# Unit 0's second-layer steps mixed with its last four first-layer steps, and another spread of steps over slots 6, 7 and 8

## The chip, the cores and the metric

The kernel runs on one core of one Trainium2 chip. The metric is the device time of one execution in microseconds (us), taken as the median of several runs. Inputs are float32, the output is float32; inside, matmul operands are float16 and sums are float32.

The engines are named as the profile names them: PE is the matrix engine (PEld its weight loads), ACT does activations, DVE elementwise work, POOL masks and issues loads, SP issues stores and transposing transfers. Each engine works through its own list of instructions in order; between engines there are only semaphores. PSUM is the accumulator memory that PE writes and ACT and DVE read.

## The reference

The reference is an attention with a forget gate, followed by a two-layer MLP on its result:

```python
scores = scale * q @ k.T + (cum_i - cum_j)      # cum: cumulative sum of log f; causal mask
attn   = softmax(scores); y = attn @ v           # 8 batches x 8 heads, 576 positions, head size 64
x = y, heads side by side                        # 4608 tokens x 512
h = x @ w_in; g = h - tanh(h); out = g @ w_out   # 512 -> 2048 -> 512
```

## The kernel before

**Units and slots.** Attention is done by head pairs: 8 batches x 4 pairs, numbered 0 to 31 (batch 0 has pairs 0 to 3, batch 1 pairs 4 to 7, and so on). The MLP is done in nine units of 512 tokens. Batch 0 (pairs 0 to 3) is computed first by a prologue of its own. From then on `slot(p, take)` (L626) does the scores of pair p, the values of pair p-1, and `take` steps of the MLP between them. The list `mlp` (L591) holds all MLP steps in the order in which they are taken, and `TAKE` (L747) says how many each slot takes, from slot 4 on. Nothing reorders the instructions afterwards: every engine's queue is the order in which the code emits them.

**A slot.** `att_items` (L602) gives its items: seven tiles of scores, s0 to s6 (`scores`, L347: matmuls into a PSUM tile `ps`, exp on ACT into `e`, a mask on POOL); after s0 the transposes of the next pair's q (`trans`, L245, "q"), after s1 the values of the pair before ("v": 30 matmuls into `av`, then on DVE `rs` twice and `xn`, L392 to L394, and two transposing transfers on SP into `XR`, L401 and L403), after s3 the transposes of the next pair's k ("k"); in slot 7 these two come later, after s2 and s4. `trans` writes one PSUM tile, which is copied into `QT` or `KT` (L261 on ACT, L263 on DVE). s3 is a small tile of 64 columns per head, `el`. LOADS adds transfers, issued from POOL (v, q and k of later batches) or SP.

After each item the slot brings the count of MLP steps up to its share: with 10 items that count, step number i*take/10, rounded down, is reached after item i. For takes of 3 and 4 below slot 8 a table, `FEW`, names the items after which one step is taken.

**Buffers that matter here.** The score tiles `ps` have two PSUM buffers, `av` one, the tile "tr" (transposes; for k of batch 1 the pool below) one. The pool `ps_m` has three: they hold `hps` (first layer), `ops` (second layer) and k's transposes of batch 1.

**The MLP steps of units 0 and 1.** `mlp1` (L440) is a first-layer step: for unit 0 it has 8 matmuls of 256 columns (L448; two hidden blocks of 128 by half of the unit's tokens), then `gate` (L412): tanh on ACT (L414) and an add on DVE (L415) into `gt`. For unit 0, steps 0 to 3 and 8 to 11 make all hidden blocks of the first 256 tokens, steps 4 to 7 and 12 to 15 those of the last 256. `mlp2` (L575) is a second-layer step: 4 matmuls of 512 columns (L581) that add to an `ops` tile of 128 tokens; four steps make a tile, after which ACT copies it to `ost` (L585) and SP stores it (L587). So second-layer steps 0 to 7 (the first 256 tokens) need first-layer steps 0 to 3 and 8 to 11 only, step 10 needs first-layer steps 12 and 13, step 11 needs 14 and 15. From unit 2 on the second layer has another form (`seven`, L518), which is not touched.

Four steps are taken before slot 4. Slots 4 to 9 take 4, 4, 4, 3, 10 and 9. So slots 4, 5 and 6 hold first-layer steps 4 to 15 of unit 0, slot 7 three second-layer steps, slot 8 ten, and slot 9 the last three of unit 0 and the first of unit 1.

Of the kernel before, what the change touches and what calls it, by code (L numbers as in the profile page):

```python
# [22 lines left out]
def kernel(  # L23
# [25 lines left out]
    NFT = DFF // P  # L49
# [538 lines left out]

    pairs = [(b, c) for b in range(B) for c in range(NPAIR)]

    mlp = [(fn, u, s) for u in range(2) for fn in (mlp1, mlp2) for s in range(NFT)]  # L591
    mlp += [(fn, u, s) for u in range(2, NU) for fn, n in ((mlp1, NFT), (seven, 14)) for s in range(n)]
    done = [0]

# [31 lines left out]
    def slot(p, take):  # L626
        items = att_items(p)
        whole, n, base = sum(c != "" for _, c in items), 0, goal[0]
        for i, (emit, what) in enumerate(items):
            emit()  # L630
            if take in FEW and p < 2 * NPAIR:
                if what in FEW[take] and not (what == "s1" and p > NPAIR) or what == "v":
                    step()
                continue
            n += what != ""
            upto(base + n * take // whole)
        goal[0] = base + take
        upto(goal[0])
# [105 lines left out]
    norm0(4)  # L744
    step()
    goal[0] = done[0]
    TAKE = [4, 4, 4, 3, 10, 9] + 7 * [8] + 4 * [8, 7, 8, 7]  # L747
    for p in range(NPAIR, len(pairs) + 1):
        slot(p, TAKE[p - NPAIR])
        if p == NPAIR:  # L750
# [30 lines left out]
```

## Time and profile before

| what | value |
|---|---|
| median of 3 runs | 346.69 us (346.17 to 346.78) |
| the profiled execution's own time | 347.59 us |
| its span, first to last instruction | 345.9 us |
| mean granted PE clock | 0.999 |
| busy share PE, PEld, DVE, ACT, POOL | 97%, 68%, 68%, 64%, 46% |
| bytes moved | 45.96 MB, mean 133 GB/s |

The profile is of one execution. Busy times of matmuls are modelled and overlap their successors by their last part; so a PE without idle time starts one group of matmuls a little before the row of the group before it ends, and the pace of PE is read from starts. The chain of waits follows the execution back from its end to what released each step. A wait is put down to the releaser that came last. In timeline rows the columns are: start, duration, engine, line, operation, result and operands, shape, count of merged instructions, and in brackets the idle time before it and its releaser.

### The profile page before, as it was taken

The numbers are of one execution on the slowest core, as the hardware profiler recorded it, in microseconds if no ns is written. First come the engines' busy times: TensorE is split into PE (matmuls) and PEld (weight loads), VectorE is DVE, ScalarE is ACT, GpSimd is POOL, SyncE is SP. The second block draws the span as 40 slices with busy tenths as digits, with TensorE's granted clock in tenths as the row PEclk, the third lists the DMA queues.
The fourth block names the chain that finished last, engine by engine and source line by source line (L and its number), as shares of the span: only waits on it lengthen the run. The fifth ranks groups of instructions, "written<-read, shape, count | busy, mean of one in ns | idle before, by whom it ended". The sixth has DMA issues, their size and how long they took to land.

```text
span 345.9 us, 8688 instructions
## 1 busy us (share of the span) xinstructions
PE 335.6 (97%) x3354; PEld 235.6 (68%) x3354; DVE 236.2 (68%) x481; ACT 222.7 (64%) x417; POOL 158.6 (46%) x318
## 2 busy tenths in 40 slices
PE   7999998999999999999999999999999999999995
PEld 3879875554555557888886568756887786486485
DVE  7486888447953498648854796378637865975973
ACT  4687986448755787568756875687568843623631
POOL 8976358655276626655486547752222210000000
PEclk9999999999999999999999999999999999999999
DMA  9999999999999999999899999998430013002002
GB/s 90 141 201 187 204 200 163 143 147 192 158 133 141 205 151 159 136 182 167 170 160 195 176 165 161 185 170 177 101 110 17 19 50 108 3 30 93 0 32 91
DMA packets 161323, 45.96 MB, mean 133 GB/s; under 512 B 141506, under 2 KB 159234, under 8 KB 161282
## 3 DMA queue, kind: packets, MB, share of 16 engines
q0 software_dynamic: 100128, 18.36, 77.8%
q1 hardware_dynamic: 61074, 26.99, 39.5%
q8 instruction: 26, 0.43, 0.5%
q14 instruction: 15, 0.12, 0.1%
q10 hardware_dynamic: 80, 0.07, 0.1%
HBM read 36.85 MB, written 9.44 MB: 134 GB/s over the span
## 4 chain that ended last, share of the span: by engine, by line
PE 86%; DVE 6%; ACT 3%; DMA 2%; issue 1%; ACTq 0%; DVEq 0%
PE hps L462 31%; PE cx L503 13%; PE cz L503 10%; PE ps L358 10%; PE ops L581 8%; PE av L386 7%; PE hps L448 2%; PE ps L300 2%; DMA XR<-xn 2%; DVE gt L415 1%; PE t L272 1%; DVE KT L263 1%; ACT e L305 1%; ACT e L367 1%; DMA snap<-in_f_dram 1%
## 5 line engine op out<-in xcount | busy, mean ns | idle before, releaser
L462 PE MATMUL hps<-XR,win 128*128 128x512 f16 (+4 forms) x640 | 125.9, 336 | 0.5 <-DMA XR<-xn 0.3
L415 DVE TENSOR_TENSOR gt<-hps,th 128x512 f16<-128x512 f32 x144 | 98.4, 688 | 39.1 <-ACT th L414 38.0
L367 ACT ACTIVATE e<-ps 128x512 f16<-128x512 f32 x168 | 98.5, 594 | 40.0 <-PE ps L358 38.6
L414 ACT ACTIVATE th<-hps 128x512 f32<-128x512 f32 x144 | 86.1, 598 | 29.5 <-PE hps L462 20.2
L377 POOL TENSOR_SCALAR_AFFINE_SELECT e<-e 128x128 f16<-128x128 f16 x162 | 55.4, 343 | 106.6 <-ACT e L367 106.1
L462 PEld LDWEIGHTS <-win 128*128 128x128 f16 x640 | 56.3, 97 | 43.7 <-issue 0.5
L358 PE MATMUL ps<-QT,KT 67*128 67x512 f16 (+1 forms) x336 | 68.8, 277 | 1.2 <-ACT e L367 0.7
L503 PEld LDWEIGHTS <-gt 128*128 128x128 f16 x560 | 52.5, 97 | 8.3 <-DVE gt L415 0.4
L358 PEld LDWEIGHTS <-KT 67*128 67x128 f16 x336 | 31.9, 98 | 22.2 <-issue 1.1
L95 POOL DMA_DIRECT2D vn<-in_v_dram x40 | 34.2, 858 | 5.1 <-DMA win<-in_moe_w_in_dram 2.0
L581 PE MATMUL ops<-wout,gt 128*128 128x512 f16 x128 | 32.6, 378 | 0.0
L386 PEld LDWEIGHTS <-e 128*128 128x128 f16 x784 | 28.0, 97 | 3.6
L496 DVE TENSOR_TENSOR snap<-cz,snap 128x512 f32<-128x512 f32 x21 | 14.5, 691 | 22.4 <-PE cz L503 7.4
L386 PE MATMUL av<-vn,e 128*128 128x65 f16 x784 | 29.2, 193 | 0.0
L503 PE MATMUL cz<-wout,gt 128*128 128x256 f16 x224 | 27.8, 272 | 0.0
L394 DVE TENSOR_TENSOR xn<-av,rs 128x640 f16<-128x640 f32 x28 | 23.1, 825 | 1.0
L503 PEld LDWEIGHTS <-sw 128*128 128x128 f16 x224 | 21.0, 97 | 3.9
L106 POOL DMA_DIRECT2D qn<-in_q_dram x25 | 21.4, 855 | 1.7 <-issue 1.7
L106 POOL DMA_DIRECT2D kn<-in_k_dram x25 | 21.4, 855 | 1.2 <-issue 1.2
L540 ACT ACTIVATE snap<-cx 128x512 f32<-128x512 f32 (+1 forms) x16 | 8.7, 544 | 16.2 <-PE cx L503 16.2
L581 PEld LDWEIGHTS <-gt 128*128 128x128 f16 x128 | 11.1, 97 | 10.6 <-issue 0.5
L305 ACT ACTIVATE e<-ps 128x512 f16<-128x512 f32 x25 | 14.4, 596 | 5.2 <-PE ps L303 3.2
(108 smaller groups left out, 378.5 us busy)
## 6 DMA issues: line engine op xcount, KB each, us to landing
vn<-in_v_dram POOLq DMA_DIRECT2D x32, 128.0 KB, 6.3
out_dram<-ost SPq DMA_DIRECT2D x14, 256.0 KB
out_dram<-snap SPq DMA_DIRECT2D x14, 256.0 KB
qn<-in_q_dram POOLq DMA_DIRECT2D x24, 128.0 KB, 5.8
kn<-in_k_dram POOLq DMA_DIRECT2D x24, 128.0 KB, 4.2
QT<-TQ SPq DMA_DIRECT2D x10, 288.0 KB
KT<-TK SPq DMA_DIRECT2D x10, 288.0 KB
win<-in_moe_w_in_dram POOLq DMA_DIRECT2D x2, 1024.0 KB, 11.2
```

Source lines behind the costliest of these rows:

```text
L95: nc.gpsimd.dma_start(out=dst[0:pn, n, h0:h1, 0:D], in_=src[b, h0:h1, n * P:n * P + pn, :].rearrange("h p d -> p h d"))
L106: nc.gpsimd.dma_start(out=to, in_=src[b, :, n * P:n * P + pn, :].rearrange("h p d -> p h d"))
L358: nc.tensor.matmul(out=ps[:, col:col + n], lhsT=KT[b % 2][0:D + 3, h, j * P:(j + 1) * P], rhs=QT[b % 2][0:D + 3, h, i0:i0 + n], start=True ...
L367: nc.scalar.activation(out=e[:, lo:hi], in_=ps[:, lo:hi], func=AF.Exp, scale=qscale)
L377: nc.gpsimd.affine_select(out=view, in_=view, compare_op=ALU.is_ge, fill=0.0, base=0, pattern=pat, channel_multiplier=-1)
L386: nc.tensor.matmul(out=av[:, a, ib, :], lhsT=E.pop((b, 2 * c + a, j, ib)), rhs=vn[b % 2][:, j, 2 * c + a, 0:D + 1], start=(j == 0), stop=( ...
L394: nc.vector.tensor_tensor(out=xn.rearrange("p i (a d) -> p a i d", a=2), in0=av[:, :, :, 0:D], in1=rs.to_broadcast([P, 2, NJ, D]), op=ALU. ...
L414: nc.scalar.activation(out=th, in_=hps, func=AF.Tanh, scale=-1.0)
L415: nc.vector.tensor_tensor(out=to, in0=view(hps), in1=view(th), op=ALU.add)
L462: nc.tensor.matmul(out=hps[:, o:o + n], lhsT=win[:, ci, ft * P:(ft + 1) * P], rhs=XR[:, ci, t:t + n], start=(ci == 0), stop=(ci == NCH - 1))
L503: nc.tensor.matmul(out=ps, lhsT=stationary(u, LHS[ph], ft, m), rhs=moving(RHS[ph], ft), start=fresh and ft == 0, stop=(ft == HF - 1), skip ...
L581: nc.tensor.matmul(out=ops, lhsT=GT[(u, ft, m)], rhs=wout[:, ft, :], start=(ft == 0), stop=(ft == NFT - 1))
```

## The change

It rewrites the first part of the list `mlp` for unit 0, and three numbers of `TAKE`.

```diff
-    mlp = [(fn, u, s) for u in range(2) for fn in (mlp1, mlp2) for s in range(NFT)]
+    mlp = [(mlp1, 0, s) for s in range(12)]
+    for i in range(4):
+        mlp += [(mlp2, 0, 4 * i), (mlp2, 0, 4 * i + 1)] + [(mlp1, 0, 12 + j) for j in ((0,), (2,), (), ())[i]]
+        mlp += [(mlp2, 0, 4 * i + 2), (mlp2, 0, 4 * i + 3)] + [(mlp1, 0, 12 + j) for j in ((1,), (3,), (), ())[i]]
+    mlp += [(fn, 1, s) for fn in (mlp1, mlp2) for s in range(NFT)]
     mlp += [(fn, u, s) for u in range(2, NU) for fn, n in ((mlp1, NFT), (seven, 14)) for s in range(n)]
...
-    TAKE = [4, 4, 4, 3, 10, 9] + 7 * [8] + 4 * [8, 7, 8, 7]
+    TAKE = [4, 4, 5, 5, 7, 9] + 7 * [8] + 4 * [8, 7, 8, 7]
```

Written M for second-layer and F for first-layer steps of unit 0, the steps with the item after which each is taken (q, v and k are the items named above) are:

| slot | before | after |
|---|---|---|
| 6 | F12 v, F13 s3, F14 s4, F15 s6 | M0 q, M1 v, F12 s3, M2 s4, M3 s6 |
| 7 | M0 v, M1 s4, M2 s6 | F13 s1, M4 s2, M5 s3, F14 k, M6 s6 |
| 8 | M3 s0, M4 q, M5 s1, M6 v, M7 s2, M8 s3, M9 k, M10 s4, M11 s5, M12 s6 | M7 q, F15 s1, M8 s2, M9 s3, M10 s4, M11 s5, M12 s6 |
| 9 | M13 to M15, then unit 1 | the same |

No instruction is added or removed on any engine; from the item s4 of slot 8 on, PE's list is the same in both. On SP, the store of the first tile of unit 0 now stands ahead of slot 7's transposing transfers, and the second store ahead of slot 8's.

## The prediction

> **What bounds the kernel now.** First the shares and the slices of the page, then who PE waited for, then PE's work by slot.
>
> ```profile
> span 345.9 us, 8688 instructions
> PE 335.6 (97%) x3354; PEld 235.6 (68%) x3354; DVE 236.2 (68%) x481; ACT 222.7 (64%) x417; POOL 158.6 (46%) x318
> PE   7999998999999999999999999999999999999995
> PEclk9999999999999999999999999999999999999999
> DMA  9999999999999999999899999998430013002002
> ```
>
> ```profile
> PE hps L448 <- DVE gt L415: 0.9, 2, 0.6
> PE ps L358 <- ACT e L367: 0.7, 2, 0.4
> PE ps L358 <- DVE KT L263: 0.4, 1, 0.4
> PE hps L462 <- DMA XR<-xn: 0.3, 1, 0.3
> ```
>
> PE bounds the kernel: 97% of the span, at full clock. So the instructions that the change moves cost nothing by being moved; what counts is the time in which PE stands. Three of the waits above lie in the slots that change. The windows are slots 6, 7 and 8 (from s0 to s0), columns: stretch, length, then busy time of PE, PEld, DVE, ACT, POOL.
>
> ```profile
> 47.63:54.72 7.09, 6.48 (x89) 5.39 (x87) 6.19 (x11) 5.89 (x13) 6.22 (x12) 1.00 1.35 195
> 54.72:61.76 7.04, 6.03 (x69) 3.35 (x67) 5.70 (x9) 4.36 (x9) 5.87 (x13) 1.00 3.85 140
> 61.76:73.21 11.45, 11.45 (x95) 6.17 (x95) 4.41 (x7) 5.19 (x10) 7.12 (x15) 1.00 1.67 148
> ```
>
> Slot 8 is full on PE and empty on DVE (4.41 of 11.45); slot 6 is the other way round (DVE 6.19 of 7.09). This is the imbalance that the change works on. PE's own rows, slot 6 and then slot 7 into 8:
>
> ```profile
> 47.86 0.42 PE L254 MATMUL t<-id,qn 96*128 96x96 f16 x6
> 48.11 0.38 PE L358 MATMUL ps<-QT,KT 67*128 67x448 f16 x2
> 48.33 0.58 PE L386 MATMUL av<-vn,e 128*128 128x65 f16 x14
> 49.24 1.04 PE L448 MATMUL hps<-XR,win 128*128 128x256 f16 x8
> 50.11 0.44 PE L358 MATMUL ps<-QT,KT 67*128 67x320 f16 x4
> 51.52 0.38 PE L358 MATMUL ps<-QT,KT 67*128 67x512 f16 x1
> 52.51 1.03 PE L448 MATMUL hps<-XR,win 128*128 128x256 f16 x8 [0.61 <-DVE gt L415]
> ...
> 57.42 0.42 PE L254 MATMUL t<-id,qn 96*128 96x96 f16 x6
> 58.32 0.38 PE L358 MATMUL ps<-QT,KT 67*128 67x512 f16 x1 [0.43 <-ACT e L367]
> 58.54 1.03 PE L581 MATMUL ops<-wout,gt 128*128 128x512 f16 x4
> 59.63 0.41 PE L254 MATMUL t<-id,kn 96*128 96x96 f16 x6
> 60.32 1.03 PE L581 MATMUL ops<-wout,gt 128*128 128x512 f16 x4
> 61.76 0.39 PE L358 MATMUL ps<-QT,KT 67*128 67x512 f16 x1 [0.41 <-DVE KT L263]
> 61.98 1.03 PE L581 MATMUL ops<-wout,gt 128*128 128x512 f16 x4
> 62.85 0.42 PE L254 MATMUL t<-id,qn 96*128 96x96 f16 x6
> ```
>
> Start to start gives the paces: a second-layer step 0.87 (61.98 to 62.85), a first-layer half step 0.87 (49.24 to 50.11), a set of transposes 0.25 (47.86 to 48.11), a score tile 0.22 (48.11 to 48.33), the values 0.91 (48.33 to 49.24), the small tile s3 0.06 (50.11 to 50.39 less 0.22 is 0.06). Without any wait the three slots are 17 steps x 0.87 = 14.8, 18 tiles x 0.22 = 4.0, three s3 0.2, six sets 1.5, three values 2.7: 23.2 us. They take 73.21 - 47.63 = 25.6. So 2.4 us are lost there, and that is the most this change can give.
>
> **The change part by part.** I follow PE through the new order with these paces and ask at each step what it waits for. Durations on the other engines:
>
> ```profile
> 51.46 0.60 ACT L414 ACTIVATE th<-hps 128x512 f32<-128x512 f32 x1
> 50.58 0.17 DVE L392 TENSOR_SCALAR rs<-av 128x10 f32<-128x10 f32 x1
> 50.79 0.22 DVE L393 RECIPROCAL rs<-rs 128x10 f32<-128x10 f32 x1
> 51.04 0.82 DVE L394 TENSOR_TENSOR xn<-av,rs 128x640 f16<-128x640 f32 x1
> 51.78 1.28 DVE L415 TENSOR_TENSOR gt<-hps,th 128x512 f16<-128x512 f32 x2
> 52.98 1.61 DVE L263 COPY KT<-t 64x576 f16<-64x576 f16 x2
> 57.87 1.61 DVE L263 COPY QT<-t 64x576 f16<-64x576 f16 x2
> ```
>
> *Slot 6.* Now M0 at 48.11, s1 48.98, values 49.20, M1 50.1, s2 and s3 51.0, F12 51.25, k 52.1, s4 52.4, M2 52.6, s5 and s6 53.5, M3 53.9, ready for slot 7's s0 at 54.79. The wait of 0.61 goes: only one `hps` is in flight. What is late next is k's copy: F12 ends at 52.3, its tanh (0.60) at 52.93, its gate holds DVE 0.6 before the two copies (1.61): 55.18, so s0 starts at 55.23. 0.44 lost, where this slot lost 0.8 (51.52 + 0.22 to 52.51) before.
>
> *Slot 7.* s0 55.23, s1 55.45, F13 55.67, values 56.55, s2 57.45, M4 57.7, q 58.5, s3 58.8, M5 58.9, s4 59.7, ready for k at 59.95. There is one "tr" buffer, so k waits until q is copied. DVE: F13 ends 56.7, tanh 57.35, gate to about 58.0 (it now stands ahead of the norm), rs, rs and xn until 59.25 (xn's end is 1.28 behind the first rs), two copies of q 1.61: 60.85. PE goes on at 61.0: 1.05 lost, where slot 7 lost about 0.2 at this place before (58.54 + 0.87 to 59.63). In return the wait on ACT goes (0.43; 0.6 by paces: M4, q and M5 now stand between s2 and s4), and so does the wait on k's copy: F14 (0.87) stands behind k, so s0 of slot 8 is ready at 63.45, and the copies, begun at 61.45, are done at 63.1. Slack 0.3.
>
> *Slot 8.* From 63.45 on, seven steps instead of ten. F15's gate falls in DVE's free time; F14's gate, on which M8's buffer waits, ends at 63.7, M8 starts at 67. No wait: 7 x 0.87 + 6 x 0.22 + 0.06 + 0.5 + 0.91 = 8.9, so slot 9 begins at 72.3 to 72.4, not 73.21.
>
> *Inputs taken earlier.* M0 to M3 read `wout` at 48.1, 50.1, 52.6 and 53.9; before, the first read is at 56.3.
>
> ```profile
> L581 PE MATMUL ops<-wout,gt x128: 377/378/382, 56.3 to 114.4; 128*128 128x512 f16 x128
> ...
> L210 POOL DMA_DIRECT2D wout<-in_moe_w_out_dram x4: 742/744/757, 31.7 to 35.9; - x4
> DMA to landing us min/median/max: 10.9/13.3/14.8
> ```
>
> The first is issued at 31.7 and lands by 46.5 even at the maximum, the last by 50.7: slack 1.6 and 3.2. Cost nothing; uncovered, each us late is a us lost.
>
> *SP's queue.* Two stores now stand ahead of transposing transfers: ready at about 55.6 and 65.6, when the norms behind them end at 59.3 and 68.6. No delay; a store held up would hold the transposes of `XR` with it (a rival below).
>
> Sum: lost before 2.4, lost after 0.44 + 1.05 = 1.5, gain 0.9; as each handover between engines costs some 0.04 more (the first rs ends at 50.75, the second starts at 50.79), I take 0.85. After slot 8 PE's list is the same and PE remains the bound (its one later wait on a transfer, the 0.3 on `XR`, begins at the end of a norm that moves along), so the gain stays to the end. The profiled execution took 347.59 (span 345.9, 1.7 around it) and would take 346.74; the median of the runs is 346.69, 0.90 below that execution, so 345.84. Bounds: every wait gone gives 344.3; nothing gained 346.7.
>
> The Trainium skill (Perfetto Trace Analysis, Optimization Strategy) says that where the most-contended engine changes over time, interleaving the regimes may improve performance. The windows agree that the regimes differ (DVE 6.19 of 7.09, then 4.41 of 11.45); taken as far as it goes, it would give 344.3, the first rival. [...]
>
> **The rivals.**
> 1. *All waits go* (0.07). If q's copies in slot 7 came before the norm or the gate, the 1.05 would go, and with it most of the rest: 344.3 to 345.1. Against it: DVE's list is fixed, gate, norm, copies.
> 2. *The new waits are larger* (0.18). Each new wait stands behind a tanh and a gate. If ACT takes F13's tanh 0.6 later (one more activation ahead of it, 0.60), k in slot 7 waits 1.65, and the gain is 0.25; the slack of 0.3 at slot 8's s0 does not help. 346.2 to 346.6.
> 3. *DMA sets the pace* (0.05). Loads for later batches come no earlier, and PE waits for them later on: 346.7.
> 4. *XR is late* (0.10). Unit 1's first step needs the transposes of slot 8's norm.
>
> ```profile
> 66.63 0.82 DVE L394 TENSOR_TENSOR xn<-av,rs 128x640 f16<-128x640 f32 x1
> 77.63 1.03 PE L462 MATMUL hps<-XR,win 128*128 128x512 f16 x4
> 145.18 5.58 DMA XR<-xn
> ```
>
> Before, xn ended at 67.45 and PE read at 77.63, 10.2 us behind it, without a wait. After, xn ends at about 68.6 (F15's gate delays it) and PE wants to read at 76.8: 8.2 us. Where PE did wait for such a transfer, later on, it took 5.58 from xn's end; nothing shows more than that it took under 10.2 here. The rival begins at 8.2, cancels the gain at 9.1 and makes the kernel measurably slower from 9.8 (the transposes of TQ follow on the same queue): 347.4.
>
> **How the numbers follow.** My forecast has 0.60, with a gain of 0.4 to 1.25: 345.4 to 346.3. A difference under 0.2% (0.69 us) is about what measuring can't tell from none. Of the 0.60, 0.48 lie above 0.69 of gain; with rival 1, faster has 0.55. Same has the rest of mine (0.12), rival 2 and rival 3: 0.35. Slower has rival 4: 0.10. The range, 345.1 to 346.8, leaves out rival 1 and rival 4, under 0.2.
>
> **What would show it.** Right: no wait of `hps` L448 near 52; s0 of slot 7 waiting 0.3 to 0.6 on DVE's KT; in slot 7 k's transposes waiting about 1 us behind DVE's QT, the longest wait after the prologue; s0 of slot 8 without a wait of note; slot 9 beginning at 72.2 to 72.6. Wrong: M0 to M3 waiting for a transfer; a wait of `hps` L462 on `XR` near 77; slot 9 at 72.4 but an end that is not earlier, which would be rival 3.

## The result

The changed kernel took 345.62 us in the median of 20 runs, the kernel before 346.74: 1.12 us less, where 0.85 was forecast. The ratio is 0.9957, with a 95% interval of 0.9940 to 0.9974, which makes a gain of 1.5 us (0.9 to 2.1). In a later comparison of 12 runs with 17 it was 0.9958 (0.9937 to 0.9979), with medians 1.09 us apart. Three executions, one each of the changed kernel (497.66 us), the kernel before (438.61) and the kernel `both` of the experiments (496.52, the profile of both_timed), ran at a mean granted clock of 0.66 to 0.75, and the ratios, unlike the medians, leave them out.

The ratio gives more than the medians, and so do the means of the same executions, which lie 1.55 and 1.41 us apart. Three of the kernel before's 20 executions took 348.6 to 350.31 us; of the other 19 of the changed kernel none took more than 346.64. No profile shows one of these long executions of the kernel before, so what makes them is open.

The profiled execution took 346.0 us, with a span of 344.3, 1.6 less than that of the kernel before.

The profile after, by the same views. First the page: shares, and DMA by slices.

```profile
span 344.3 us, 8688 instructions
PE 334.6 (97%) x3354; PEld 235.2 (68%) x3354; DVE 236.2 (69%) x481; ACT 222.9 (65%) x417; POOL 158.6 (46%) x318
DMA  9999999999799999999999999999330013002002
```

Then who PE waited for, as far as it differs or belongs to the change (columns: total us, times, longest).

```profile
PE t L254 <- DVE QT L263: 0.8, 1, 0.8
PE ps L358 <- DVE KT L263: 0.3, 1, 0.3
PE hps L448 <- DVE gt L415: 0.3, 1, 0.3
PE ps L358 <- ACT e L367: 0.2, 1, 0.2
```

The second wait of `hps` L448 (0.6, near 52.5) is gone, the wait of `ps` on ACT in slot 7 is gone, and a new wait, k's transposes on q's copies, is the longest after the prologue. Slots 6, 7 and 8 by windows (stretch, length, busy time of PE, PEld, DVE, ACT, POOL):

```profile
47.42:55.00 7.58, 7.29 (x80) 4.53 (x79) 5.56 (x9) 5.64 (x12) 6.12 (x12) 1.00 1.42 172
55.00:63.15 8.15, 7.34 (x83) 4.95 (x83) 5.27 (x9) 4.59 (x10) 6.58 (x13) 1.00 2.53 160
63.15:72.01 8.86, 8.86 (x88) 5.39 (x87) 5.34 (x9) 5.68 (x11) 6.59 (x13) 1.00 2.39 156
sum 24.59, PE 23.49 PEld 14.87 DVE 16.18 ACT 15.91 POOL 19.29; mean PE 7.83 PEld 4.96 DVE 5.39 ACT 5.30 POOL 6.43
```

They take 24.59 us, where they took 25.58 (47.63 to 73.21): 0.99 less. DVE's work is now about the same in all three slots. The PE rows and the DVE rows of the two waits that were forecast:

```profile
53.69 1.03 PE L581 MATMUL ops<-wout,gt 128*128 128x512 f16 x4
55.00 0.61 PE L358 MATMUL ps<-QT,KT 67*128 67x512 f16 x3 [0.29 <-DVE KT L263]
59.49 0.38 PE L358 MATMUL ps<-QT,KT 67*128 67x512 f16 x1
60.69 0.42 PE L254 MATMUL t<-id,kn 96*128 96x96 f16 x6 [0.81 <-DVE QT L263]
63.15 0.38 PE L358 MATMUL ps<-QT,KT 67*128 67x512 f16 x1
72.01 0.38 PE L358 MATMUL ps<-QT,KT 67*128 67x512 f16 x1
```

```profile
57.15 0.69 DVE L415 TENSOR_TENSOR gt<-hps,th 128x512 f16<-128x512 f32 x1 [2.21 <-ACT th L414]
57.76 0.16 DVE L392 TENSOR_SCALAR rs<-av 128x10 f32<-128x10 f32 x1
57.95 0.22 DVE L393 RECIPROCAL rs<-rs 128x10 f32<-128x10 f32 x1
58.20 0.82 DVE L394 TENSOR_TENSOR xn<-av,rs 128x640 f16<-128x640 f32 x1
58.94 1.60 DVE L263 COPY QT<-t 64x576 f16<-64x576 f16 x2
```

The gate of F13, the norm and the two copies of q follow each other without a gap, and PE goes on 0.15 behind their end (60.54).

**Where the rest of the 1.6 us of the profiled pair is.** Each execution can be cut into the prologue up to s0 of slot 6, slots 6 to 8, and the rest:

| | slot 6 begins | slots 6 to 8 | rest |
|---|---|---|---|
| before | 47.63 | 25.58 | 272.69 |
| after | 47.42 | 24.59 | 272.29 |
| difference | 0.21 | 0.99 | 0.40 |

Up to slot 6 the programs are equal, so 0.21 is not the change's doing by its order of work. In the rest, the one difference in PE's waits is the wait of 0.25 on `XR` near 150.8 (about 0.4 by paces), which the kernel before has and the changed one has not. The experiments look at both.

### The profile page after: what moved, and what is told of

Its sections match the earlier page's. It is cut to its first block, busy times and chain, and to the rows that moved or that the text cites. A ratio compares the mean times of both kernels' runs of the same rounds, so it can differ in the third digit from the quotient of the medians.

```text
span 344.3 us, 8688 instructions
## 1 busy us (share of the span) xinstructions
PE 334.6 (97%) x3354; PEld 235.2 (68%) x3354; DVE 236.2 (69%) x481; ACT 222.9 (65%) x417; POOL 158.6 (46%) x318
## 4 chain that ended last, share of the span: by engine, by line
PE 88%; DVE 5%; ACT 4%; POOL 1%; issue 1%; DMA 1%; ACTq 0%; DVEq 0%
PE hps L462 31%; PE cx L503 14%; PE cz L503 11%; PE ps L358 10%; PE ops L581 7%; PE av L386 7%; PE hps L448 2%; PE ps L300 2%; DVE gt L415 1%; PE t L272 1%; ACT e L305 1%; DVE QT L263 1%; ACT e L367 1%; ACT th L414 1%; PE av L313 1%
## 5 line engine op out<-in xcount | busy, mean ns | idle before, releaser
L503 PEld LDWEIGHTS <-gt 128*128 128x128 f16 x560 | 52.5, 97 | 8.2 <-DVE gt L415 0.4
```

The source lines that it names most:

```text
L503: nc.tensor.matmul(out=ps, lhsT=stationary(u, LHS[ph], ft, m), rhs=moving(RHS[ph], ft), start=fresh and ft == 0, stop=(ft == HF - 1), skip ...
```

## The experiments

All edits are against the kernel named. "Slots 6 to 8" is the time from s0 of slot 6 to s0 of slot 9 in the profile; ratios are to the kernel before on the same chip.

**b_again: the kernel before, unchanged, in a second profile.**

> The kernel before, profiled once more. Question: slots 6 to 8 became 0.99 us shorter, yet the profiled spans differ by 1.6: 0.21 was there before slot 6, where the programs are equal, and 0.42 at the wait for XR near 150.8. Theory A (chance): these 0.6 us are scatter between executions; here slots 6 to 8 take 25.6 us again (25.5 to 25.7), but the start of slot 6 or the wait for XR lies elsewhere by 0.1 us or more. Theory B (the new order causes them through the transfers): slot 6 starts at 47.6 and the wait of 0.25 on XR is there again.

Slot 6 began at 46.73, slots 6 to 8 took 26.51 (to 73.24), the span was 345.5. Slots 6 to 8 did not take 25.6, and the wait on `XR` was not there. PE's waits and rows show why; below them are the chain of waits (start, length, what) up to this point, and the load's row in the first profile of the kernel before, the last number being the us from issue to landing:

```profile
PE t L254 <- DMA kn<-in_k_dram: 1.0, 1, 1.0
...
59.65 0.43 PE L254 MATMUL t<-id,kn 96*128 96x96 f16 x6 [0.99 <-DMA kn<-in_k_dram]
61.79 0.39 PE L358 MATMUL ps<-QT,KT 67*128 67x512 f16 x1 [0.41 <-DVE KT L263]
73.24 0.38 PE L358 MATMUL ps<-QT,KT 67*128 67x512 f16 x1
...
39.18 20.43 DMA kn<-in_k_dram
...
kn<-in_k_dram POOLq DMA_DIRECT2D x1, 576.0 KB, 18.6
```

Both theories missed something. The load of batch 2's k, issued in slot 4, landed at 59.6, and slot 7's k transposes could not start earlier. This execution came out of the prologue 0.9 earlier than the first one, and lost that again at the load: k's transposes at 59.65 and 59.63, slot 9 at 73.24 and 73.21. In the first profile the load landed at 57.2 (issued 38.61, 18.6 to landing), so there it was not what held PE.

**take_alone: only the takes.** Against the kernel before:

```diff
-    TAKE = [4, 4, 4, 3, 10, 9] + 7 * [8] + 4 * [8, 7, 8, 7]
+    TAKE = [4, 4, 5, 5, 7, 9] + 7 * [8] + 4 * [8, 7, 8, 7]
```

> Only TAKE is changed (5, 5, 7), the list stays as before, unmixed. Theory A (what counts is that PE has more work in slots 6 and 7, whichever steps they are): by paces slot 9 starts 24.4 to 24.8 us behind slot 6 (before 25.58, after 24.59), the gain is that of the whole change, ratio to before 0.995 to 0.998. Theory B (the mix of second- and first-layer steps does it): waits of hps on gates come back, slots 6 to 8 take 25.2 to 25.6 and the ratio is 0.999 to 1.001.

The median was 345.57, the ratio 0.9955 (0.9931 to 0.9978). Slots 6 to 8 took 24.75 (46.77 to 71.52). PE's rows:

```profile
52.27 1.03 PE L448 MATMUL hps<-XR,win 128*128 128x256 f16 x8 [0.35 <-DVE gt L415]
60.25 0.41 PE L254 MATMUL t<-id,kn 96*128 96x96 f16 x6 [0.65 <-DVE QT L263]
71.52 0.38 PE L358 MATMUL ps<-QT,KT 67*128 67x512 f16 x1
```

The unmixed list with the new takes gains 0.83 of the 0.99: the wait on a gate stays, at 0.35 instead of 0.61, and slot 7 waits only for q's copies. Theory A holds: it is the takes that count.

**list_alone: only the mixed list.** Against the changed kernel:

```diff
-    TAKE = [4, 4, 5, 5, 7, 9] + 7 * [8] + 4 * [8, 7, 8, 7]
+    TAKE = [4, 4, 4, 3, 10, 9] + 7 * [8] + 4 * [8, 7, 8, 7]
```

> Only the list is mixed, TAKE stays 4, 3, 10 in slots 6 to 8. Theory A (the takes do it): the wait of hps at 52.5 goes, but slot 7 has three steps between its items as before and waits on ACT (0.7) and, with F13's gate ahead of k's copies, on KT at slot 8's s0 (up to 1.4): slots 6 to 8 take 25.3 to 26.0, ratio 0.999 to 1.002. Theory B (the mix does it): 24.5 to 24.9, ratio 0.995 to 0.998.

The median was 347.08, the ratio 1.0012 (0.9983 to 1.0040); slots 6 to 8 took 26.01 (46.60 to 72.61).

```profile
56.96 0.38 PE L358 MATMUL ps<-QT,KT 67*128 67x512 f16 x1 [0.64 <-ACT e L367]
61.14 0.39 PE L358 MATMUL ps<-QT,KT 67*128 67x512 f16 x1 [1.35 <-DVE KT L263]
```

The wait at 52.5 went, and came back as 1.35 at s0 of slot 8, behind F13's gate and k's copies, as forecast. The mix by itself gains nothing. On top of the takes it is worth 0.16 us of the slots, by one profile of take_alone and three of the changed kernel, which gave 24.59, 24.59 and 24.60; the times of the two (ratios 0.9955 and 0.9957) can't be told apart.

**k_buffer: k's transposes of slot 7 in another PSUM tile.** Against the changed kernel:

```diff
-        if b == 1 and src is kn:
+        if src is kn and (b == 1 or (b, c) == (2, 0)):
             t32 = ps_m.tile([P, UW], FP32, tag="m", name="t32")
```

> The changed kernel, with the transposes of k in slot 7 put into a tile of ps_m, so that they need not wait until q's tile is copied. Theory A (the wait of 0.81 there, 0.98 by paces, is what is left of slot 7's loss and nothing is behind it): k starts at 59.7 instead of 60.7, KT's copies still follow q's on DVE and end at 62.2, just when s0 of slot 8 is ready; slots 6 to 8 take 23.6 to 23.8, ratio to before 0.992 to 0.995. Rival (KT's copies were what counted): s0 of slot 8 waits for them instead, 24.3 to 24.6 as in the changed kernel, ratio 0.995 to 0.997.

Slots 6 to 8 took 23.69 (46.67 to 70.36); the median was 345.43, the ratio 0.9937 (0.9902 to 0.9973). k's transposes start without a wait:

```profile
57.57 0.42 PE L254 MATMUL t<-id,qn 96*128 96x96 f16 x6
58.97 0.42 PE L254 MATMUL t<-id,kn 96*128 96x96 f16 x6
61.49 0.39 PE L358 MATMUL ps<-QT,KT 67*128 67x512 f16 x1
70.36 0.38 PE L358 MATMUL ps<-QT,KT 67*128 67x512 f16 x1
```

So the single buffer was what made k wait for q's copies, and 0.90 comes back. The ratio's interval overlaps that of the changed kernel. Without the wait PE comes to k at 58.97, and the load had landed at 57.8; a landing at 59.6, as in b_again, would be waited for, so in some executions a part of the 0.90 would go again. That is read from these rows and was not run.

**f12_early: F12 one place earlier in slot 6.** Against the changed kernel:

```diff
+    mlp[13], mlp[14] = mlp[14], mlp[13]
     mlp += [(fn, 1, s) for fn in (mlp1, mlp2) for s in range(NFT)]
```

> The changed kernel with F12 one place earlier in slot 6 (M0, F12, M1, M2, M3), so that its gate lies on DVE before k's copies arrive. Theory A (the gate between k's transposes and their copies makes slot 7's s0 wait): that wait of 0.29 (0.44 by paces) goes, slot 7 begins 7.15 to 7.3 us behind slot 6 instead of 7.58, slots 6 to 8 take 24.2 to 24.4. Rival (it is only moved into slot 7's wait for q's copies, which hangs on F13's gate): F13 moves along with PE, so no; if so, 24.5 to 24.6. Ratio to before 0.993 to 0.9965.

The wait at slot 7's s0 went; slot 7 began 7.14 behind slot 6 (47.90 to 55.04), slots 6 to 8 took 24.29 (to 72.19). The median was 345.28, the ratio 0.9925 (0.9895 to 0.9955). Here the wait for `XR` is there again, 0.22 us at 149.75, and the rest took 272.61.

```profile
55.04 0.69 PE L358 MATMUL ps<-QT,KT 67*128 67x512 f16 x3
60.87 0.41 PE L254 MATMUL t<-id,kn 96*128 96x96 f16 x6 [0.87 <-DVE QT L263]
149.75 0.30 PE L462 MATMUL hps<-XR,win 128*128 128x320 f16 x1 [0.22 <-DMA XR<-xn]
```

**both: the two edits together.**

> The changed kernel with both: k's transposes of slot 7 in a tile of ps_m, and F12 one place earlier. Without waits slots 6 to 8 would take 23.2. With k_buffer alone they took 23.69. Theory A (the waits are independent): 23.25 to 23.4, no wait of PE above 0.1 us from slot 6 to slot 8; ratio to before 0.990 to 0.9945, faster than the changed kernel by 0.9 to 1.3 us. Rival (KT's copies in slot 7 become the limit): s0 of slot 8 waits 0.2 to 0.4, 23.5 to 23.7.

Slots 6 to 8 took 23.37 (50.65 to 74.02), next to 23.2 without any wait, and PE has no wait above 0.1 us in them. This execution's prologue lasted until 50.65, almost three us longer than any other's. In it the granted clock was 0.62 from 8.6 to 26.0 us and PE got 203 matmuls done, where the first profile of the kernel before has 1.00 and 241. So its span of 346.3 says nothing of the edits. The median was 345.37, the ratio 0.9930 (0.9903 to 0.9956); f12_early, whose slots are 0.92 longer, had 0.9925, so the times do not resolve the single edits.

```profile
50.65 0.38 PE L358 MATMUL ps<-QT,KT 67*128 67x512 f16 x1
65.16 0.39 PE L358 MATMUL ps<-QT,KT 67*128 67x512 f16 x1
74.02 0.38 PE L358 MATMUL ps<-QT,KT 67*128 67x512 f16 x1
```

**a_again: the changed kernel in a second profile.**

> The changed kernel, profiled once more. Theory A: slots 6 to 8 take 24.6 us again (24.5 to 24.7) wherever slot 6 begins, since k's load lands before 59.5 and PE comes to it later than that; no wait on DMA in these slots, and the wait for XR near 149 is there or not. If slot 6 begins at 46.7, as in four of the six profiles so far, PE wants k at 58.8 and starts at 60.0 behind q's copies: a load landing up to 60 costs nothing.

Slots 6 to 8 took 24.59 again (47.21 to 71.80), with the wait of 0.82 behind q's copies and none on DMA; no wait on `XR`. k's load landed at 57.2 here (38.51 and 18.7) and at 58.4 in the first profile of this kernel (37.80 and 20.6).

**b_k_early: the kernel before with batch 2's q and k loaded earlier.**

```diff
-    LOADS = {(NPAIR, 5): [lambda: load_qk(qn, q, 2, 0, H)],
-             (NPAIR, 6): [lambda: load_qk(kn, k, 2, 0, H)]}
+    LOADS = {(NPAIR, 0): [lambda: load_qk(qn, q, 2, 0, H)],
+             (NPAIR, 1): [lambda: load_qk(kn, k, 2, 0, H)]}
```

> The kernel before, with batch 2's loads of q and k issued after s0 and s1 of slot 4 instead of s5 and s6 (about 1 us earlier on POOL's queue). In the second look at the kernel before, k's load landed at 59.6 and PE waited 0.99 us for it at 59.65; in the first look it landed at 57.2 and PE started these transposes at 59.63 without that wait. Theory A (the kernel before loses up to 1 us at this load in part of its executions, which the changed kernel, arriving there 1 us later with two more steps done, does not): k lands at 56 to 58.7, no wait of L254 on DMA, slots 6 to 8 take 25.5 to 25.6 us, and the median falls: ratio 0.996 to 0.9985. Theory B (the load's wait is rare, the extra gain is chance): ratio 0.999 to 1.001.

k's load was issued at 38.70, only 0.5 earlier than in b_again, and landed at 57.5; slot 7 did not wait for it, and slots 6 to 8 took 25.59 (46.78 to 72.37). The median was 346.64, the ratio 0.9976 (0.9949 to 1.0004). The ratio is where theory A put it, but the interval takes in no change. The edit also hardly moved the load: in the ten profiles with the load at its place and usable rows, k was issued at 37.8 to 39.3. So this stays open.

**b_k_late and a_k_late: both kernels with these loads later, k's by five to seven us.** Against the kernel before and the changed kernel:

```diff
-    LOADS = {(NPAIR, 5): [lambda: load_qk(qn, q, 2, 0, H)],
-             (NPAIR, 6): [lambda: load_qk(kn, k, 2, 0, H)]}
+    LOADS = {(NPAIR + 1, 0): [lambda: load_qk(qn, q, 2, 0, H)],
+             (NPAIR + 1, 2): [lambda: load_qk(kn, k, 2, 0, H)]}
```

> The kernel before, with batch 2's loads of q and k issued after s0 and s2 of slot 5 instead of s5 and s6 of slot 4, some 3 us later. With 18 to 20 us to landing k would arrive at 60.5 to 62. Theory A (slots 6 to 8 of the kernel before hang on this load as soon as it lands later than about 58.7 to 59.6): PE waits for k's load 1.0 to 3.0 us in slot 7, slots 6 to 8 take 26.6 to 28.5 us, and slot 9 begins at 74.1 to 75.6 whatever the prologue took. Theory B (the wait seen once was something else): 25.6.

> The changed kernel with the same later loads. Theory A (the changed kernel needs k 1 us later with two more steps done, and its wait behind q's copies covers part of the load): slots 6 to 8 take 24.6 to 26.5, and the two kernels now differ in these slots by 1.5 to 2.3 us instead of 0.99. Theory B: they differ by 0.99 as before.

In the kernel before, k's load landed at 60.33 (chain of waits: start, length, what), PE waited 1.80 for it, and slots 6 to 8 took 27.36 (46.61 to 73.97):

```profile
44.23 16.10 DMA kn<-in_k_dram
60.33 0.05 issue
60.38 0.44 PE t L254 x6
```

In the changed kernel they took 24.59 (47.66 to 72.25), with 0.81 behind q's copies and no wait on the load. The two differ by 2.77, more than the 1.5 to 2.3 that theory A gave. But the loads did not land alike: in the changed kernel k was issued at 45.28 and was there after 12.8, at 58.1. So the pair shows that the kernel before pays for a late load about one to one (a wait of 1.80, and slots 1.78 longer than in its first profile), and that the changed one went on unharmed with a load issued at 45.3; it does not show what the changed kernel would pay for a landing at 60.3. By its rows PE goes on to k at 60.9 in that execution, so a landing up to then would cost nothing; that is argued, not run.

**a_timed and both_timed: the changed kernel and `both`, side by side.**

> The changed kernel timed beside the next one on the same chip. Theory A: slots 6 to 8 24.6 us; ratio to before 0.994 to 0.9975, which is the 0.99 of the slots and a part of the up to 0.9 that the kernel before loses at k's load.

> k_buffer and F12 early together, once more, beside the changed kernel. In the profile its slots 6 to 8 took 23.37 against 24.59. Theory A (what is gained in these slots stays to the end, the prologue's scatter aside): median 0.7 to 1.5 us under that of the changed kernel. Rival (some of it is given back, as k's load now binds: PE comes to k at 58.0 to 58.9, when it lands at 57.2 to 59.6): 0.2 to 0.7 us under.

The changed kernel took 346.16 in the median of 12 runs, ratio 0.9958 (0.9937 to 0.9979); slots 6 to 8 took 24.60 in its profile. `both` took 344.98 in the median of 6, ratio 0.9919 (0.9888 to 0.9950). It is 1.2 us under the changed kernel, where its slots are shorter by 1.22; the intervals still overlap by 0.0013, so that it is faster is likely and not shown beyond doubt. No row of its profile is used.

## Why the prediction was right, and where its size was off

*What bounds.* Right: PE is still busy for 97% of the span with the same 3354 matmuls, and what changed in these slots were its waits.

*Slot 6.* Forecast: the wait on the gate goes, and slot 7's s0 waits for k's copies, 0.44 by paces, 7.60 behind slot 6. Measured: 7.58, with a wait of 0.29 in the row (0.44 by paces: M3 began at 53.69, s0 at 55.00). f12_early shows that the place of F12's gate made it.

*Slot 7.* Forecast: k held behind gate, norm and q's copies, 1.05 by paces, and no wait at slot 8's s0. Measured: k at 13.27 behind slot 6 (forecast 13.4), 0.98 by paces (59.49 + 0.22 to 60.69), and s0 of slot 8 at 15.73 (forecast 15.8) without a wait. k_buffer shows that the one PSUM tile made it.

*Slot 8.* Forecast 8.9 us, measured 8.86. Slot 9 was to begin at 72.3 to 72.4 with slot 6 at 47.63, so 24.7 to 24.8 behind; it was 24.59. The handovers for which the sum had taken off a little were not there.

*Inputs and SP.* `wout` was there at each of its four reads: PE has no wait on it. On SP the two stores started at 55.37 and 65.31, and the transposing transfers behind them at 59.05 and 68.31, within 0.05 of xn's ends (59.02 and 68.28); the stores held nothing up. DVE's and PE's rows at the end of slot 8 and the start of unit 1:

```profile
67.46 0.82 DVE L394 TENSOR_TENSOR xn<-av,rs 128x640 f16<-128x640 f32 x1
76.42 1.03 PE L462 MATMUL hps<-XR,win 128*128 128x512 f16 x4
```

xn of slot 8 ended at 68.28 and unit 1 read at 76.42 without a wait, so these transfers took at most 8.1 us in place of the 10.2 known before, and the rival of a late `XR` at this place did not come.

*The sum.* 0.99 in the slots stands against 0.85, and it came again within 0.01 in two further profiles of the changed kernel. The whole kernel gained 1.1 us by the medians and 1.5 by the ratio. The mis-sized term is the loss before: slots 6 to 8 were taken to lose 2.4 us, from one execution in which k's load landed at 57.2, and this was called the most that the change can give. "Inputs taken earlier" looked only at `wout`, which the change reads earlier, and at no input that it reads later. Of that kind is k: the changed kernel comes to it two steps later and then stands behind q's copies anyway, so it did not wait for the load in any of its profiles, while the kernel before lost 0.99 in its row there in one of two profiles (and slots 6 to 8 took 0.93 longer). That a late load costs this is shown by b_again and b_k_late.

How much of the gain this makes is not shown. The kernel before wants k about 12.0 us behind s0 of slot 6: with slot 6 at 46.73, q's copies end at 56.96 + 1.61, and PE goes on 0.15 later. Of the ten landings with the load at its place only that of b_again lies later behind its own slot 6 (12.9 us; the others 7.0 to 11.7). By so few it is about 0.1 us in the mean (an estimate: 0.9 in one of ten), which is the distance of the medians from 0.99. b_k_early's gain of 0.24% has an interval that takes in zero. So 0.99 is shown; 0.1 us above it would fit this load, and the rest up to the 1.5 of the ratio, to which the long executions of the kernel before belong, is open.

*`XR` near 150.* The wait was there in two of the thirteen profiles that can be used (before, f12_early), where the rest took 272.6 to 272.7; without it the rest took 272.2 to 272.5. It came in one of two profiles of the kernel before and in none of three of the changed one. Whether the change has a part in it stays open.

*The rivals.* That all waits go was wrong for this change; `both` comes close to it (23.37 in these slots, where the kernel before took 25.58). Larger waits did not come. That DMA sets the pace was wrong as it was put, that nothing could be gained; but one transfer did set the pace of slot 7 in the kernel before, in one of its two profiles. The rule of the Trainium skill (Perfetto Trace Analysis, Optimization Strategy) on interleaving regimes held in direction: DVE's busy times in the three slots went from 6.19, 5.70 and 4.41 to 5.56, 5.27 and 5.34, and the slots became 0.99 shorter. The experiments divide the credit: the takes, which even out PE's and DVE's work over the slots, gave 0.83, the mix of steps inside a slot 0.16, and the mix alone lost 0.43.

## What to carry to other kernels

Where an engine is bound and its waits are short, walk its order with start-to-start paces and ask at each step who is late: that gave each of two new waits within 0.1 us. Then ask of the kernel before, not only of the new one, which inputs arrive at a time of their own, and look at more than one execution of it: a load that lands within a us of its use is a cost in some executions only, and a change that moves the use back takes it away unseen. A buffer that two transposes share is worth looking at when the copies out of it stand behind other work: a second tile gave back 0.90 us in these slots.

## What the runs showed of the hardware

The same prologue took from 46.6 to 47.9 us up to slot 6 in twelve profiles, and 50.65 in one, whose granted clock was 0.62 from 8.6 to 26.0 us; in the twelve it was 0.90 to 1.00 there. The load of batch 2's k (576 KB), issued at 37.8 to 39.3, took 18.4 to 20.6 us and landed at 57.2 to 59.6; issued five to seven us later, at 45.3 and 44.2, it took 12.8 and 16.1 and landed at 58.1 and 60.3. A later issue thus cost less than its delay. At the 205 GB/s that all transfers together moved from 36 to 46 us in b_k_late, 576 KB alone would take 2.9 us (an estimate), so it seems that most of the time to landing goes to other transfers; no run shows this apart. DMA stood at nine tenths or more in nearly every slice up to 240 us in both kernels, while PE, with the loads at their place, lost at most one us in these slots to a transfer. Busy shares of the DMA engines alone thus decided nothing here; who waited for a transfer did.
